# Fused attention and two networks on one core: the second network's down product as seven products of 256 columns, spread over three items

## The chip, the cores and the metric

The kernel runs on one core of one Trainium2 chip, as one launch. The metric is the device time of the launch in microseconds. Five engines work in a core: PE multiplies matrices (its weight loads are shown apart, as PEld), DVE, ACT and POOL do elementwise work, and SP here only issues the transfers (DMA). Matrix products end in PSUM, which this kernel uses as eight buffers (banks) of 512 float32 columns; DVE or ACT carries them from there to SBUF.

## The reference, cut to what matters

```python
x = attention(q, k, v)                 # 2304 tokens, 512 features, chunks of 64 tokens
P = sinkhorn(exp(x @ w_gate))          # 8 experts, 8 rounds
out = sum_e P[:, e] * (relu(x @ w1[e]) @ w2[e])        # first network, 1024 hidden each
h = maximum(maximum(out @ w1, out @ w2), out @ w3)     # second network, 768 hidden
return h @ w_out                                       # the down product of the change
```

All is float32 in and out. The kernel splits each operand of a product into a high part and a low remainder (both of the type float32r) and adds three products: high by high, high by low, low by high.

## The kernel before, in words

**Items.** The work is a list of 123 items (`items`). Items 0 to 95 are the first network, items 96 to 122 (kind `m`) the second: for each of three blocks of 768 tokens (`sb`) three parts `p` of 256 hidden units, and for each part three items `i`, one for each of the weights w1, w2 and w3. Three items with i = 0, 1, 2 make a group: the elementwise maximum of their three results is the hidden tile, `m`, of four quarters (two halves of the hidden units by two halves of the tokens, the tokens alternating by q = 0, 1).

**The up product.** `up(n)` computes an item by seven products instead of eight, after Strassen and Winograd: `PRODUCTS` lists them with the bank (`a`, `g`, `b`) into which each is added. A position `pos` (0 to 6) is one such product: 2 k by 3 parts, so 6 matmuls of 384 columns, 42 an item. After positions 0, 1 and 2 ACT copies the bank aside (`s0` to `s2`, line 360), after positions 3 to 6 DVE adds and takes the maximum (lines 366 and 313). The next product on the same bank waits for that read.

**The down product.** `down(n, q, j)` (line 452) multiplies one of six token tiles of 128 tokens by w_out: 6 matmuls of 512 columns, accumulated in one bank of the pools `wk` and `dn`, and `evict2` (line 493) copies or adds the bank to `ar`; with the last part `p` it sends the tile to `out`. The six tiles of a group (36 matmuls) run in one piece after position 6 of the next group's first item; those of the very last group run at the end, with two left over from the group before it.

**Weights.** All weights of the second network stand prepared in DRAM, `scr` (up) and `scro` (down). They pass through a ring of 24 slots of 256 KB in SBUF (`wr`). `line_up_all` fixes the order of the chunks, 7 slots for each item and 4 for each group's down product, and `room(k)` gives back k slots and issues the next chunks that fit. SP issues in the order of the program and each transfer waits there, so a transfer that waits holds all that stand behind it.

**The next block's input.** `x_next` (line 675) loads two token tiles of the next block (`xr`), and `x_cols` (line 571) turns them into the seven moving operands in three steps; its first step has ACT casts and DVE subtractions that read `xr`. Six such pieces run in items 98 to 113, one in a group, and `xcol` holds them.

**Decoding.** During the first network's blocks 1 and 2, `decode_all` (line 724) turns the second network's float64 weights into the prepared form, a step at a time, by `decode_step`.

**What sets the order.** All is written out by hand in the loop at line 1207: `at(n, pos, fn)` places side work behind a position, `later` holds splits for the next position, `pend` the tiles of the down product. Each engine runs its own list in that order.

Of the kernel before, what the change touches and what calls it, by code (L numbers as in the profile page):

```python
# [9 lines left out]
F32 = mybir.dt.float32  # L10
F32R = mybir.dt.float32r
# [37 lines left out]
DOWN = ["c0", "t1", "t2", "t3", "c1", "c3", "t4"]  # L49


@with_exitstack
def kernel(ctx: ExitStack, tc: tile.TileContext, qk, vv, wg, wts, wts2, out):
# [31 lines left out]
    scr = dram.tile([3 * NP2, P, 7, 2, 2, P], F32, name="scr")  # L85
    scro = dram.tile([NP2, P, 2, 2, DM], F32, name="scro")
    w1s = dram.tile([NPAIR, P, 7, 512], F32, name="w1s")
# [141 lines left out]
    def line_up(key, src, n, parts):  # L229
# [5 lines left out]
        slot_of[key] = []  # L235

    def line_up_all():
        for n in range(NPAIR, ni):
            it = items[n]
            if n == NPAIR:  # L240
                continue
            if it["kind"] == "M":
                line_up(("U", n), w1s[it["g"]], 7, (4, 3))
            else:
                line_up(("U", n), scr[it["p"] * 3 + it["i"]].rearrange("p s h k f -> p s (h k f)"), 7, (4, 3))
            if NPAIR + 2 <= n < first_of[3] + 2:
                j = (n - NPAIR - 2) // 2
                key, o = ("D", j), w2s[j % NPR].rearrange("p s b f -> p (s b) f")
                if n % 2 == 0:
                    line_up(key, o[:, 0:6], 6, (4, 2))  # L250
                else:
                    line_up(("E", j), o[:, 6:14], 8, (4, 4))
            elif n >= first_of[3] + 2 and it["i"] == 0 and n > first_of[3]:
                line_up(("O", n - 1), scro[items[n - 1]["p"]].rearrange("p c h f -> p (c h) f"), 4, (4,))
        line_up(("O", ni - 1), scro[items[ni - 1]["p"]].rearrange("p c h f -> p (c h) f"), 4, (4,))

    def room(k):
        ring["room"] += k
        while chunks and chunks[0][2] <= ring["room"]:
            key, a, k, src = chunks.pop(0)  # L260
            ring["room"] -= k
            while k:
                s = ring["put"] % NSLOT
                m = min(k, NSLOT - s)
                nc.sync.dma_start(out=wr[:, s:s + m].bitcast(F32).rearrange("p s h f -> p s (h f)"),
                                  in_=src[:, a:a + m])
                slot_of[key] += range(s, s + m)
                ring["put"] += m
                a, k = a + m, k - m

# [4 lines left out]

    mt = [None]
    later = []

    def up(n):
# [8 lines left out]
        if m2 and it["i"] == 0:  # L288
            c = mt[0] = pbm.rearrange("p b q w -> p (b q) w")
        if it["down"] and not scaled:  # L290
            hb = hr[:, (it["p"] if m2 else n) % 2]
            hh, hl = hb[:, 0], hb[:, 1]
            it["h"] = (hh, hl)

        def finish(q, src):
# [17 lines left out]
            nc.vector.tensor_tensor(out=m[:, q], in0=src, in1=m[:, q], op=ALU.max)  # L313
            if it["i"] == 2:
                lo = lambda: nc.vector.tensor_tensor(
                    out=hl[:, q], in0=m[:, q], in1=hh[:, q].bitcast(F32), op=ALU.subtract)
                later.append(lambda: (nc.scalar.copy(out=hh[:, q], in_=m[:, q]), later.append(lo)))

        def scale(out, src, pb):
# [132 lines left out]
    def down(n, q, j):  # L452
# [7 lines left out]
        own_w = own(n)  # L460
        o = p.rearrange("p (a b) -> p a b", a=2) if own_w else p
        for f in range(2):
            hi = HIDX[f, q]
            for i, (h, x) in enumerate(((hh, 0), (hh, 1), (hl, 0))):
                if own_w:
                    w = w2b(n)[:, 2 * f:2 * f + 2, x]
                else:
                    w = wr[:, slot_of["O", n][2 * f + x]].rearrange("p h f -> p (h f)")
# [4 lines left out]
    def new_acc(t):  # L473
        acc[t] = ar[:, t % TS]
        return acc[t]

    def evict(it, t, p):
# [12 lines left out]
        if it["g"] == NPAIR - 1:  # L490
            y_due.append((clock[0], t))

    def evict2(it, t, p):
        if it["p"] == 0:
            nc.scalar.copy(out=new_acc(t), in_=p)
            return
        nc.vector.tensor_tensor(out=acc[t], in0=p, in1=acc[t], op=ALU.add)
        if it["p"] == NP2 - 1:
            nc.sync.dma_start(out=out[t * P:(t + 1) * P, :], in_=acc[t])

# [181 lines left out]
    def big_again():  # L682
# [3 lines left out]
        big[0] = ctx.enter_context(tc.tile_pool(name="big2", bufs=1, reuse_waits="tile"))  # L686
        xb.extend(big[0].tile([P, 7, 2, W], F32R, name=nm) for nm in ("xbh", "xbl"))


# [34 lines left out]
    def decode_all(half_):  # L724
        jobs = []
        for p in range(NP2):
# [5 lines left out]
            for c in range(2):  # L732
                jobs.append((p, None, c, [(slice(0, 4), wts2[2 * (2 * p + c) + 1, :, 1].rearrange(
                    "p (i f) -> p i f", i=4))]))
        m = len(jobs) // 2
        jobs = jobs[m * half_:m * half_ + m]
        loaded, rest = {}, []
        for at_ in range(-1, m):
# [13 lines left out]
            nc.gpsimd.tensor_tensor(out=V[:, 0:4].rearrange("p i f -> p (i f)"), in0=v, in1=r, op=ALU.add)  # L752
            hi, lo = (bg_[:, o:o + 896].bitcast(F32R).rearrange("p (i f) -> p i f", i=7) for o in (4096, 4992))
            yield
            if i is not None:
                strassen_w([V[:, x] for x in range(4)], [V[:, 4 + x] for x in range(4)], nc.gpsimd)
                src = V[:, 1:8]
                dst = lambda h, p=p, i=i, k=k: scr[p * 3 + i, :, :, h, k, :]
            else:
                hi, lo = (x[:, 0:4].rearrange("p i f -> p (i f)") for x in (hi, lo))  # L760
                src = V[:, 0:4].rearrange("p i f -> p (i f)")
                dst = lambda h, p=p, k=k: scro[p, :, k, h]
            yield
            nc.scalar.copy(out=hi, in_=src)
            yield
            rest = [lambda lo=lo, src=src, hi=hi: nc.vector.tensor_tensor(
                        out=lo, in0=src, in1=hi.bitcast(F32), op=ALU.subtract),
                    lambda lo=lo, hi=hi, dst=dst: [nc.sync.dma_start(out=dst(h), in_=x.bitcast(F32))
                                                   for x, h in ((hi, 0), (lo, 1))]]
            if at_ + 1 < m:  # L770
# [269 lines left out]
    def s_open():  # L1040
# [8 lines left out]
        views.append(left.tile([P, NH - 13, 2, W], F32R, name="hy"))  # L1049
        bg_ = left.tile([P, 5888], F32, name="bg")  # L1050
        views.append(hr.rearrange("p b h q w -> p (b h q w)").rearrange("p (s h w) -> p s h w", h=2, w=W))
# [42 lines left out]
    for k in (4, 5):  # L1094
        for j in range(TS // 2):
            n = first_of[k - 1] + 3 * j
            if k == 4 and j < 2:
                n = first_of[3] + 3 + j
                if j == 0:
                    at(n - 1, 0, lambda n=n: x_next(4, 0, n))  # L1100
                else:
                    for a in (2, 9, 15):
                        at(n + a // 7, a % 7, lambda n=n: next(xcol[n]))
# [12 lines left out]
    with tc.manual_schedule():  # L1116
# [87 lines left out]

        held = [((7 * n + 6 + i) // 7, (7 * n + 6 + i) % 7) for n in (NPAIR, NPAIR + 1) for i in range(3)]
        pend = [(0, q, j) for q in (1, 0) for j in range(TS // 2)]
        for n in range(1, ni):
# [3 lines left out]
            for pos in up(n):  # L1211
# [18 lines left out]
                if pos < 3:  # L1230
                    decode_step(n)
                if n <= NPAIR:
                    run = 2 if pos in (1, 3, 5) else 0
                else:
                    run = len(pend) if pos == 6 and big_m and it["i"] == 0 else 0
                    if run and n > ni - 4:
                        run = 4
                for i in range(run):
                    if pend:
                        down(*pend.pop(0))  # L1240
                    while pos == 5 and later:
                        later.pop(0)()
                    if n in xcol and n != first_of[3] + 4 and i in (0, 2, 4):
                        next(xcol[n])
                    if (n, i) == (first_of[3] + 3, 3):
                        x_next(4, 1, n + 1)
                if run and big_m and not pend:
                    room(4)
                if pos == 3 + (n == 1):
# [17 lines left out]
            if it["down"] and (n < NPAIR or big_m):  # L1267
                assert len(pend) == (2 if n == ni - 1 else 0)
                pend += [(n, q, j) for q in (1, 0) for j in range(TS // 2)]
        while later:  # L1270
            later.pop(0)()
        for d in pend:
            down(*d)
# [39 lines left out]
```

## Time and profile before

| | |
|---|---|
| median of 3 runs | 1774.05 us (1773.16 to 1775.4) |
| the profiled execution's own time | 1772.81 us |
| its span, first to last instruction | 1771.0 us |
| PE busy | 1761.3 us, 99% of the span |
| DVE, POOL, ACT busy | 73%, 56%, 44% |
| granted TensorE clock | 1.00 of 2.4 GHz in nearly all of the span |

The span is what the profiler saw of that one execution; about 1.8 us of its time lie around it. A view of windows gives the busy time of each engine in a stretch, a timeline the instructions in order, the view of waits who waited for whom. A matmul's duration in a timeline holds its way through the array, so the time that one costs in a stream is read from the starts of a row of them.

### The profile page before, as it was taken

How to read it: one execution, taken by the hardware profiler on the slowest of the kernel's cores; microseconds unless marked ns; L12 is line 12 of the kernel's file. 1: busy time of each engine (PE TensorE's matmuls, PEld its weight loads, DVE VectorE, ACT ScalarE, POOL GpSimd, SP SyncE). 2: the span in 40 equal slices, each digit the busy share in tenths (PEclk: the TensorE clock that was granted, in tenths of full speed). 3: DMA queues.
4: the chain of work that ended last, by engine and by line, in shares of the span. 5: the costliest groups of instructions: out<-in, count | busy, mean ns of one | idle time of the engine just before them, and what ended most of it. 6: DMA issues, size and time to landing. Idle time of an engine off the chain costs nothing.

```text
span 1771.0 us, 30169 instructions
## 1 busy us (share of the span) xinstructions
PE 1761.3 (99%) x10764; PEld 1682.9 (95%) x10764; DVE 1298.7 (73%) x2342; ACT 777.1 (44%) x1566; POOL 997.5 (56%) x891
## 2 busy tenths in 40 slices
PE   8999999999999999999999999999999999999999
PEld 7888888989999999999999999999999999999998
DVE  8768657678885778887886886878788766664535
ACT  6665664664555534333333444434333333323221
POOL 4665665677777776766675677576767555000000
PEclk9999999999999999999999999999999999999999
DMA  7999998899988888988889779888988786877662
GB/s 240 364 368 358 334 357 309 326 373 338 357 309 334 326 315 285 335 299 298 286 311 319 255 259 345 305 298 294 318 302 315 266 304 244 282 254 260 244 245 106
DMA packets 206487, 532.89 MB, mean 301 GB/s; under 512 B 16161, under 2 KB 95361, under 8 KB 181249
## 3 DMA queue, kind: packets, MB, share of 16 engines
q1 hardware_dynamic: 206336, 530.97, 83.8%
q8 instruction: 85, 1.39, 0.3%
q14 instruction: 66, 0.53, 0.1%
HBM read 373.31 MB, written 156.02 MB: 299 GB/s over the span
## 4 chain that ended last, share of the span: by engine, by line
PE 97%; DMA 1%; DVE 1%; ACT 1%; issue 0%; POOL 0%; SPq 0%; DVEq 0%; POOLq 0%
PE pa L353 28%; PE dn L411 27%; PE dn L469 19%; PE pg L353 14%; PE pb L353 7%; DMA w2s<-w2y 0%; PE xp L905 0%; PE s L804 0%; DMA st<-in_wts 0%; PE gp L922 0%; PE hq L660 0%; PE hs L804 0%; DVE xl L602 0%; POOL wr L170 0%; PE yp L506 0%
## 5 line engine op out<-in xcount | busy, mean ns | idle before, releaser
L353 PE MATMUL pa<-xh,wr 128*128 128x384 f32 x1808 | 529.6, 337 | 0.0
L469 PE MATMUL dn<-wr,hr 128*128 128x512 f32 x1476 | 356.2, 392 | 0.0
L353 PEld LDWEIGHTS pa<-xh,wr 128*128 128x128 f32 x1808 | 332.5, 188 | 5.6 <-DVE c L366 0.8
L469 PEld LDWEIGHTS dn<-wr,hr 128*128 128x128 f32 x1476 | 275.4, 188 | 53.9
L353 PE MATMUL pa<-xl,wr 128*128 128x384 f32 x904 | 303.1, 335 | 0.0
L411 PE MATMUL dn<-hr,wr 128*128 128x384 f32 x1344 | 274.9, 335 | 0.0
L353 PE MATMUL pg<-xh,wr 128*128 128x384 f32 x904 | 268.4, 337 | 0.1
L360 ACT COPY s<-pa 128x384 f32<-128x384 f32 x244 | 117.3, 481 | 301.4 <-PE pa L353 297.4
L411 PEld LDWEIGHTS dn<-hr,wr 128*128 128x128 f32 x1344 | 237.1, 188 | 0.1
L366 DVE TENSOR_TENSOR c<-pb,s 128x384 f32<-128x384 f32 x82 | 45.7, 557 | 201.8 <-PE pb L353 179.6
L273 POOL TENSOR_TENSOR hr<-c,hr 128x384 fp32r<-128x384 f32 x96 | 110.9, 1161 | 143.0 <-ACT hr L272 137.7
L411 PE MATMUL dn<-hx,wr 128*128 128x384 f32 x840 | 182.8, 338 | 0.0
L353 PEld LDWEIGHTS pa<-xl,wr 128*128 128x128 f32 x904 | 169.7, 188 | 4.0
L353 PEld LDWEIGHTS pg<-xh,wr 128*128 128x128 f32 x904 | 166.4, 188 | 1.8 <-DVE tq L322 0.3
L353 PE MATMUL pg<-xl,wr 128*128 128x384 f32 x452 | 151.1, 334 | 0.0
L411 PEld LDWEIGHTS dn<-hx,wr 128*128 128x128 f32 x840 | 151.0, 188 | 0.0
L273 POOL TENSOR_TENSOR hr<-tq,hr 128x384 fp32r<-128x384 f32 x128 | 148.0, 1172 | 0.5 <-ACT hr L272 0.5
L353 PE MATMUL pb<-xh,wr 128*128 128x384 f32 x452 | 134.1, 337 | 0.0
L420 DVE TENSOR_TENSOR ar<-dn,ar 128x384 f32<-128x384 f32 x240 | 122.8, 545 | 9.4 <-PE dn L411 9.2
L273 POOL TENSOR_TENSOR hx<-c,hx 128x384 fp32r<-128x384 f32 x60 | 68.7, 1148 | 106.2 <-ACT hx L272 105.7
L411 PE MATMUL dn<-hy,wr 128*128 128x384 f32 x504 | 111.1, 336 | 0.0
L420 DVE TENSOR_TENSOR ax<-dn,ax 128x384 f32<-128x384 f32 x180 | 93.2, 549 | 18.2 <-PE dn L411 18.2
(246 smaller groups left out, 3208.5 us busy)
## 6 DMA issues: line engine op xcount, KB each, us to landing
wr<-w2s SPq DMA_DIRECT2D x80, 1024.0 KB, 6.4
w1s<-wr SPq DMA_DIRECT2D x32, 1792.0 KB, 9.8
wr<-w1s SPq DMA_DIRECT2D x53, 1024.0 KB, 7.6
wr<-w1s SPq DMA_DIRECT2D x58, 768.0 KB, 6.7
w2s<-wr SPq DMA_DIRECT2D x55, 512.0 KB, 6.6
wr<-w2s SPq DMA_DIRECT2D x52, 512.0 KB, 7.1
wr<-scr SPq DMA_DIRECT2D x22, 1024.0 KB, 5.1
wr<-scr SPq DMA_DIRECT2D x27, 768.0 KB, 6.0
```

Source lines behind the costliest of these rows:

```text
L273: (eng or nc.gpsimd).tensor_tensor(out=l, in0=v, in1=h.bitcast(F32), op=ALU.subtract)
L353: nc.tensor.matmul(ps, lhsT=wt[:, x, ws], rhs=y[:, xi, k], start=b not in begun, stop=k == 1 and i == 2, skip_group_check=True)
L360: nc.scalar.copy(out=s[pos], in_=ps)
L366: nc.vector.tensor_tensor(out=inner, in0=ps, in1=s[other], op=ALU.add)
L411: nc.tensor.matmul(p, lhsT=w[:, a, dt * P:(dt + 1) * P], rhs=h[m][:, b], start=m == 0 and q == 0, stop=m == 1 and q == 2)
L420: nc.vector.tensor_tensor(out=o, in0=p, in1=o, op=ALU.add)
L469: nc.tensor.matmul(o, lhsT=h[:, hi, ts], rhs=w, start=(f == 0 and i == 0), stop=(f == 1 and i == 2))
```

## The change

It replaces the down product of the second network, for all groups but the last, by the same seven-product scheme as the up product: seven products of 3 matmuls of 256 columns for each pair of token tiles (j = 0, 1, 2), which `token_down` yields one by one. They are no longer run in one piece but spread over the three items of the next group, by `TURNS` (key 7 * i + pos, value the pairs j that make a step there). The four sums of hidden quarters that the scheme needs are taken on DVE and split on ACT and POOL (7 splits where there were 4 quarters). The down weights become seven prepared sums (`scro` of 7 or 8 slots instead of 4); they stay in slots of their own (`own_o`), which are refilled behind the last step of a group, and the ring for the up weights shrinks to 17 slots. The last group keeps the old scheme.

```diff
+TOKEN = [("c0", "a"), ("t1", "g"), ("t2", "a"), ("c3", "b"), ("t3", "a"), ("c1", "g"), ("t4", "a")]
+HSLOT = {"c0": 0, "t1": 1, "t2": 2, "c3": 4, "t3": 5, "c1": 6, "t4": 7}
+TURNS = {4: (0,), 5: (0,), 6: (0,), 7: (0,), 8: (0,), 9: (0,), 10: (0, 1), 11: (1, 1), 12: (1,), 13: (1,),
+         14: (1, 2), 15: (1,), 16: (2, 2), 17: (2, 2), 18: (2,), 19: (2,)}
...
-                line_up(("O", n - 1), scro[items[n - 1]["p"]].rearrange("p c h f -> p (c h) f"), 4, (4,))
-        line_up(("O", ni - 1), scro[items[ni - 1]["p"]].rearrange("p c h f -> p (c h) f"), 4, (4,))
+                if n == first_of[3] + 3:
+                    line_up(("O", n - 1), flat(scro[items[n - 1]["p"]]), 7, (4, 3))
+        slot_of["O", ni - 1] = []
...
+            got = []
+            for _ in range(k):
+                got.append(ring["put"])
+                ring["put"] = min((s - got[-1] - 1) % NSLOT + got[-1] + 1 for s in range(NSLOT) if s not in own_o) % NSLOT
+            slot_of[key] += got
+            fetch(got, src[:, a:a + k])
+            if key == ("O", first_of[3] + 2):
+                own_o.extend(got)
...
+            if it["i"] == 2 and n < ni - 1:
+                if q.start == 3:
+                    t = mq[0]
+                    at(n + 1, 0, lambda: (sub(t[:, 0], m[:, 2], m[:, 0]), sub(t[:, 1], m[:, 1], t[:, 0])))
+                    at(n + 1, 1, lambda: (split("t1", t[:, 0]), sub(m[:, 2], m[:, 1], m[:, 2])))
...
+    def token_down(n, j):
+        it = items[n]
+        slots, first_, last = slot_of["O", n], it["p"] == 0, it["p"] == NP2 - 1
+        t = it["sb"] * TS + 2 * j
+        turn[0] ^= 1
+        pools = {"a": (wk, dn)[turn[0]], "g": (dn, wk)[turn[0]], "b": (wk, dn)[turn[0]]}
+        C = lambda d, q, t=t: ar[:, (t + q) % TS, 256 * d:256 * d + 256]
+        bank = {}
+        for x, (kind, b) in enumerate(TOKEN):
+            fresh = b not in bank
+            if fresh:
+                pl = pools[b]
+                bank[b] = pl.tile([P, DM], F32, name="dn", tag=pl.name)[:, 0:256]
+            ps, h, w = bank[b], hr8[:, HSLOT[kind]], wr[:, slots[OSLOT[kind]]]
+            for i, (y, z) in enumerate(((0, 0), (0, 1), (1, 0))):
+                nc.tensor.matmul(ps, lhsT=h[:, y, j * P:(j + 1) * P], rhs=w[:, z],
+                                 start=fresh and i == 0, stop=i == 2, skip_group_check=True)
+            if x < 3:
+                o = C(*((0, 0), (1, 1), (0, 1))[x])
+                if first_:
+                    nc.scalar.copy(out=o, in_=ps)
+                else:
+                    e = big[0].tile([P, 256], F32, name=f"e{x}", tag=f"e{x}")
+                    nc.scalar.copy(out=e, in_=ps)
+                    nc.gpsimd.tensor_tensor(out=o, in0=o, in1=e, op=ALU.add)
+            else:
+                o = C(*((0, 0), (1, 1), (0, 1), (1, 0))[x - 3])
+                if x == 6 and first_:
+                    nc.scalar.copy(out=o, in_=ps)
+                else:
+                    nc.vector.tensor_tensor(out=o, in0=ps, in1=o, op=ALU.add)
+            if last and x >= 5:
+                q = 6 - x
+                nc.sync.dma_start(out=out[(t + q) * P:(t + q + 1) * P, :], in_=ar[:, (t + q) % TS])
+            if j == TS // 2 - 1 and x == 6 and n + 3 < ni - 1:
+                slot_of["O", n + 3] = own_o
+                for a, b in ((0, 4), (4, 7)):
+                    fetch(own_o[a:b], flat(scro[items[n + 3]["p"]])[:, a:b])
+            yield
...
+            for a in (7, 9, 10) if (k, j) == (4, 1) else (6, 9, 10):
+                at(n + a // 7, a % 7, lambda n=n: next(xcol[n]))
...
-                for i in range(run):
+                for _ in range(2 if n <= NPAIR and pos in (1, 3, 5) else 0):
                     if pend:
                         down(*pend.pop(0))
...
+                if nets:
+                    for j in TURNS.get(7 * it["i"] + pos, ()):
+                        if n < ni - 1 or pos < 3:
+                            next(nets[j])
...
         while later:
             later.pop(0)()
+        for _ in nets[-1]:
+            pass
+        turn[0] ^= 1
         for d in pend:
             down(*d)
```

The left-out rest makes `decode_all` write the seven sums (four more POOL subtractions for each of its six down pieces), gives `fetch` its loop, and adds the tiles `mq`.

On SP, around the start of the group of items 102 to 104, where `xr` of block 1 is fetched (`wr` is the ring, `scr` the up weights, `scro` the down weights, 512 columns a slot), there stood before:

```order
L265 DMA wr<-scr 128x1536
L265 DMA wr<-scro 128x2048
L265 DMA wr<-scr 128x2048
L265 DMA wr<-scr 128x1536
L265 DMA wr<-scr 128x2048
L679 DMA xr<-ys 128x512 x2
L265 DMA wr<-scr 128x1536
```

At the same place stands now:

```order
L285 DMA wr<-scr 128x1536
L285 DMA wr<-scro 128x2048
L285 DMA wr<-scro 128x1536
L285 DMA wr<-scr 128x512
L285 DMA wr<-scr 128x1536 x2
L749 DMA xr<-ys 128x512 x2
L285 DMA wr<-scr 128x2048
```

The down weights, 4 slots before and 7 now, have moved from inside a group to its border, directly ahead of the 7 slots of the next item but one and of `xr`.

On ACT, around the casts of `xr` in item 108 (line 495 before and 546 now evict a down product's bank, `s` an up product's), there stood before:

```order
L360 COPY s_16749<-pg 128x384
L360 COPY s_16758<-pa 128x384
L311 COPY pbm<-pa 128x384
L495 COPY ar<-dn 128x512
L581 CAST xh<-xr 128x4x128
L582 CAST xh<-xr 128x2x128
L495 COPY ar<-dn 128x512 x2
```

There stands now, in the same item:

```order
L332 COPY pbm<-pa 128x384
L651 CAST xh<-xr 128x4x128
L652 CAST xh<-xr 128x2x128
L546 COPY ar<-dn 128x256
L395 COPY s_17087<-pa 128x384
L395 COPY s_17101<-pg 128x384
```

The casts stand at the same position, but behind them now come an eviction of the bank `a` of the down product and the copies of the next item's up product.

On DVE, at the end of the program, there stood before:

```order
L366 TENSOR_TENSOR c<-pg,s_17871 128x384
L313 TENSOR_TENSOR pbm<-c,pbm 128x384
L313 TENSOR_TENSOR pbm<-pa,pbm 128x384
L315 TENSOR_TENSOR hr<-pbm,hr 128x768
L315 TENSOR_TENSOR hr<-pbm,hr 128x384 x2
L497 TENSOR_TENSOR ar<-dn,ar 128x512 x8
```

And now:

```order
L401 TENSOR_TENSOR c<-pg,s_18463 128x384
L334 TENSOR_TENSOR pbm<-c,pbm 128x384
L334 TENSOR_TENSOR pbm<-pa,pbm 128x384
L346 TENSOR_TENSOR hr<-pbm,hr 128x768
L346 TENSOR_TENSOR hr<-pbm,hr 128x384 x2
L556 TENSOR_TENSOR ar<-dn,ar 128x256 x4
L568 TENSOR_TENSOR ar<-dn,ar 128x512 x6
```

Between the last hidden tile and the last six tiles stand now the evictions of four steps of `token_down` that the last item did not take.

## Rows read from the trace of the kernel before

**Rows 1.** The page's head: span, then busy time, share and instructions by engine.
```profile
span 1771.0 us, 30169 instructions
PE 1761.3 (99%) x10764; PEld 1682.9 (95%) x10764; DVE 1298.7 (73%) x2342; ACT 777.1 (44%) x1566; POOL 997.5 (56%) x891
```
**Rows 2.** The chain of waits that ended last, shares of the span.
```profile
PE 97%; DMA 1%; DVE 1%; ACT 1%; issue 0%; POOL 0%; SPq 0%; DVEq 0%; POOLq 0%
```
**Rows 3.** Windows, second network: length, busy by engine, clock, DMA share, GB/s.
```profile
1487.00:1771.00 284.00, 280.26 (x1511) 266.74 (x1509) 151.20 (x263) 79.32 (x156) 6.14 (x3) 1.00 0.66 233
```
**Rows 4.** PE's timeline around one group's down product: start, length, engine, line, operation.
```profile
1585.60 8.36 PE L469 MATMUL dn<-wr,hr 128*128 128x512 f32 x36
1593.80 0.33 PE L353 MATMUL pa<-xbh,wr 128*128 128x384 f32 x1
...
1594.86 0.33 PE L353 MATMUL pg<-xbh,wr 128*128 128x384 f32 x1
...
1602.15 0.33 PE L353 MATMUL pg<-xbh,wr 128*128 128x384 f32 x1
```
**Rows 5.** Weight loads' timeline in the attention's start, products of 128 columns.
```profile
22.87 0.97 PEld L660 LDWEIGHTS hs<-xr,st 128*128 128x128 f32 x8
```
**Rows 6.** POOL groups by shape: a split of 384 columns, an add of 256.
```profile
L273 POOL TENSOR_TENSOR hr<-c,hr 128x384 fp32r<-128x384 f32 x96 | 110.9, 1161 | 143.0 <-ACT hr L272 137.7 <-issue 4.8
...
L130 POOL TENSOR_TENSOR ws<-st 128x256 f32<-128x256 f32 x32 | 27.8, 870 | 0.0
```
**Rows 7.** DMA issues of the last stretch: count, size, median us to landing.
```profile
wr<-scr SPq DMA_DIRECT2D x20, 1024.0 KB, 5.1
...
out<-ar SPq DMA_DIRECT2D x18, 256.0 KB, 2.3
...
xr<-ys SPq DMA_DIRECT2D x12, 256.0 KB, 5.4
```
**Rows 8.** A window inside a burst of transfers, columns as in Rows 3.
```profile
1611.00:1616.00 5.00, 5.00 (x30) 4.95 (x30) 2.64 (x6) 0.79 (x3) 0.00 (x0) 1.00 1.01 409
```
**Rows 9.** SP's timeline at a group's border.
```profile
1601.67 7.24 SPq L265 DMA_DIRECT2D wr<-scr  x3
1609.00 0.86 SPq L679 DMA_DIRECT2D xr<-ys  x2
```
**Rows 10.** Waits of the last stretch: us in total, times, longest.
```profile
SPq L265 <- PE pa L353: 141.1, 40, 6.9
...
DVE xT L577 <- DMA xr<-ys: 2.1, 1, 2.1
```
**Rows 11.** DVE's timeline, same border: the first read of `xr`.
```profile
1615.37 0.41 DVE L577 TENSOR_TENSOR xT<-xr 128x256 f32<-128x256 f32 x1
```
**Rows 12.** Groups by shape of the last stretch, ACT and DVE.
```profile
L360 ACT COPY s<-pa 128x384 f32<-128x384 f32 x52 | 24.9, 480 | 103.0 <-PE pa L353 98.9 <-DVE pbm L313 3.9 <-ACT hr L317 0.2
...
L581 ACT CAST xh<-xr 128x512 fp32r<-128x512 f32 x3 | 1.9, 623 | 0.0
L582 ACT CAST xh<-xr 128x256 fp32r<-128x256 f32 x3 | 1.2, 407 | 0.0
...
L577 DVE TENSOR_TENSOR xl<-xr,xh 128x256 fp32r<-128x256 f32 x3 | 1.2, 417 | 0.0
```
**Rows 13.** Timeline of PE and DVE around position 5 of an item i = 2.
```profile
1747.67 0.34 PE L353 MATMUL pg<-xh,wr 128*128 128x384 f32 x1
...
1748.54 0.55 DVE L366 TENSOR_TENSOR c<-pg,s 128x384 f32<-128x384 f32 x1
...
1749.60 0.55 DVE L313 TENSOR_TENSOR pbm<-pa,pbm 128x384 f32<-128x384 f32 x1
```
**Rows 14.** Timeline of PE and DVE at the end.
```profile
1756.18 11.08 PE L469 MATMUL dn<-wr,hr 128*128 128x512 f32 x48
...
1756.89 0.55 DVE L313 TENSOR_TENSOR pbm<-pa,pbm 128x384 f32<-128x384 f32 x1
1757.36 1.88 DVE L315 TENSOR_TENSOR hr<-pbm,hr 128x768 fp32r<-128x768 f32 x3
```

More of the change, by code (lines that the diff above doesn't have):

```diff
@@ L261, in room, with fetch @@
             ring["room"] -= k
[L262 to L269, printed above, removed]
+            got = []
[6 more added lines that the diff above has]
+                own_o.extend(got)
+    def fetch(slots, src):
+        a = 0
+        while a < len(slots):
+            k = next((k for k in range(1, len(slots) - a) if slots[a + k] != slots[a] + k), len(slots) - a)
+            nc.sync.dma_start(out=wr[:, slots[a]:slots[a] + k].bitcast(F32).rearrange("p s h f -> p s (h f)"),
+                              in_=src[:, a:a + k])
+            a += k
+    own_o = []
     def hilo(h, l, v, eng=None):
@@ L288, in up @@
         if m2 and it["i"] == 0:
-            c = mt[0] = pbm.rearrange("p b q w -> p (b q) w")
-        if it["down"] and not scaled:
-            hb = hr[:, (it["p"] if m2 else n) % 2]
+            c = mt[0] = mq[1] if mq and (n - first_of[3]) // 3 % 2 else pbm.rearrange("p b q w -> p (b q) w")
+        if it["down"] and not scaled and (not m2 or n == ni - 1):
+            hb = hr[:, 0 if m2 else n % 2]
             hh, hl = hb[:, 0], hb[:, 1]
@@ L687, in big_again @@
         xb.extend(big[0].tile([P, 7, 2, W], F32R, name=nm) for nm in ("xbh", "xbl"))
+        mq.extend(big[0].tile([P, 3 + i, W], F32, name=f"mq{i}") for i in range(2))
     big, bigs = [None], ExitStack()
@@ L752, in decode_all @@
             nc.gpsimd.tensor_tensor(out=V[:, 0:4].rearrange("p i f -> p (i f)"), in0=v, in1=r, op=ALU.add)
-            hi, lo = (bg_[:, o:o + 896].bitcast(F32R).rearrange("p (i f) -> p i f", i=7) for o in (4096, 4992))
+            hi, lo = (bg_[:, o:o + 1024].bitcast(F32R).rearrange("p (i f) -> p i f", i=8) for o in (4096, 5120))
             yield
[L755 to L762, printed above, removed]
+            strassen_w([V[:, x] for x in range(4)], [V[:, 4 + x] for x in range(4)], nc.gpsimd)
+            put = [(slice(1, 8), slice(0, 7)), (slice(0, 1), slice(7, 8))][:1 + (i is None and p == NP2 - 1)]
+            dst = scr[p * 3 + i, :, :, :, k, :] if i is not None else scro[p, :, :, :, k * P:k * P + P]
+            r = slice(2 - len(put), 8)
             yield
-            nc.scalar.copy(out=hi, in_=src)
+            nc.scalar.copy(out=hi[:, r], in_=V[:, r])
             yield
[L766 to L769, printed above, removed]
+            rest = [lambda lo=lo, V=V, hi=hi, r=r: nc.vector.tensor_tensor(
+                        out=lo[:, r], in0=V[:, r], in1=hi[:, r].bitcast(F32), op=ALU.subtract),
+                    lambda lo=lo, hi=hi, dst=dst, put=put: [
+                        nc.sync.dma_start(out=dst[:, o, h], in_=x[:, i].bitcast(F32))
+                        for i, o in put for x, h in ((hi, 0), (lo, 1))]]
             if at_ + 1 < m:
@@ L1266 @@
                 big_again()
-            if it["down"] and (n < NPAIR or big_m):
-                assert len(pend) == (2 if n == ni - 1 else 0)
+            if it["down"] and (n < NPAIR or n == ni - 1):
                 pend += [(n, q, j) for q in (1, 0) for j in range(TS // 2)]
+            elif it["down"] and big_m:
+                nets[:] = [token_down(n, j) for j in range(TS // 2)]
         while later:
             later.pop(0)()
+        for _ in nets[-1]:
+            pass
+        turn[0] ^= 1
         for d in pend:
```

58 lines of the change are left out of this document (27 added, 31 removed).

## The prediction

> **What bounds the kernel now.** I read the page's head first, then the chain of waits, then windows over the last stretch, and then timelines of one group of items, engine by engine. The reader is to see that PE is busy for 99% of the span [rows 1] and makes 97% of the chain [rows 2], so that a matmul taken away is time gained as long as nothing else comes late. In the second network (1487 to 1771 us) PE is still busy for 280 of 284 us, while DVE is at 53%, ACT at 28%, POOL nearly idle, and the transfers run at 233 GB/s [rows 3]. That mean hides something: inside a burst they run at 409 GB/s with every DMA engine busy [rows 8], so they come in bursts with pauses between, and the question is what stands behind a burst. The timelines of one group border answer it: SP waits for a slot most of the time (141 us in 40 waits for PE alone) [rows 10] and then issues the weights and `xr` [rows 9]. `xr` is issued from 1609.00 and read first at 1615.37 [rows 9, 11], about 7 us after the start of its item (1602.15 - 1.04 + 7.29 = 1608.4). It lands 5.4 us after its issue in the median [rows 7], and once in this stretch DVE already waited 2.1 us for it [rows 10]. That is the one place with no slack.
>
> **The matmuls.** In a row of them, 36 of 512 columns take 1593.80 - 1585.60 = 8.20 us, 0.2278 each, and 42 of 384 columns take 1602.15 - 1594.86 = 7.29 us, 0.1736 each [rows 4]. The straight line through both gives 0.1194 for 256 columns. Eight groups change: 8 x 36 x 0.2278 = 65.6 us go, 8 x 63 x 0.1194 = 60.2 us come, together -5.4 us. That is all the gain there is, 0.3% of the kernel, because seven products of 256 columns are 12.5% fewer columns but pay the fixed part of a matmul 63 times instead of 36. No row shows a float32r matmul of 256 columns. Below, the price is bounded by the weight loads: eight loads of 128 columns follow each other in 0.97 us, between 0.111 and 0.121 apiece [rows 5]; at 0.111 the gain is 9.6 us. Above, by the shortest spacing that this operand type shows, 0.1736: then the change costs 21.9 us. I take 0.1194, since it is nearest to the loads' own rate and lies on the line.
>
> **The side work.** A group gets seven POOL splits of at most 1.16 us and up to nine POOL adds of 0.87 us [rows 6], 16 us on an engine that was nearly idle there, in groups of some 29 us; the splits are placed two to three positions (over 2 us) ahead of their matmuls. DVE's evictions of 256 columns take 0.42 us [rows 12] where 512 columns were carried before, and it loses the four quarters' subtractions. The extra sums while decoding, 24 POOL operations of 128 columns, at most 0.87 us each, lie beside hundreds of us of PE. I cost all of it at nothing; the cover is the next position's 1.04 us of up product, and PE itself is the engine that would show it if it were gone.
>
> **The tail.** Here a stall comes in. At the end PE's up product is through at 1756.18, and DVE is busy with the last hidden tile until 1757.36 + 1.88 = 1759.24 [rows 14], 3.06 us later. Before, 12 matmuls of the group ahead (2.7 us) and tiles that need only the first quarters covered this. Now four steps x3 to x6 are left; x3 to x5 take 9 x 0.119 = 1.07 us, and x6 adds into bank `a`, which DVE has to empty of x4 first. DVE's order puts x3's and x4's adds behind the three subtractions, 0.42 us each [rows 12], so x4's is done 3.9 us after the up product. PE waits from 1.07 to 3.9: +2.8 us. The six tiles of the last group come after it unchanged.
>
> **The border with the weights' burst.** Set t = 0 where PE ends the last step (position 5 of item i = 2). The slots of the down weights are free only then, so their 7 slots (1.84 MB) are issued at t = 0, SP holds everything behind them, and then come the 7 slots of the item i = 1 and the two halves of `xr`. The first 1 MB lands at 5.1 [rows 7] and is needed at 1.04 + 5 x 1.04 = 6.25: in time. Behind it stand 0.79 + 1.84 + 0.26 = 2.88 MB, 7.05 us at 409 GB/s [rows 8], so `xr` has landed at 12.15 (first half) and 12.8 (second). That they land in order I read from the sizes: 256 KB lands after 2.3 us by itself (`out`) and after 5.4 us behind 1 MB (`xr`) [rows 7]. ACT reaches the casts of `xr` at t = 9.05 (1.04 + 7.29 + two steps) and stands there; queued behind them are the eviction of step x2 and the copies of the next item. Casts of 0.62 and 0.41 us [rows 12] end at 13.2, the eviction (256 columns, taken as 0.41) at 13.6. PE wants bank `a` for x4 after position 1 of item i = 1, at 1.04 + 8.37 + 2 x 1.04 + 0.36 = 11.85. It waits 1.75 us. Four borders have both bursts (items 102, 105, 108, 111): +7.0 us. Bounds: nothing, if the transfers overtake; and at a sixth less than 409 GB/s, 341, the 2.88 MB take 8.45 us and each border 1.4 us more.
>
> The Trainium skill ("DMA: Bandwidth & Descriptors", Specifications) puts the limit of a core's share of HBM at about 358 GB/s. By it the burst would take 8.0 us and the change cost some 5 us more than by the measured 409; the trace decides, since this core's window ran above that limit.
>
> **The border after a block's end.** In two groups (105 and 114) the finished tiles are sent to `out` ahead of the down weights on SP, and the last of them waits for DVE. Position 5 ends on PE at p = 1747.84 [rows 13]; DVE is two operations behind, and the add of x6 would start where the third starts, p + 1.76, and end at p + 2.2. With the issue of `out` the weights go out at p + 2.6 instead of p + 0.4. They land at p + 7.7, wanted at p + 6.6: 1.1 us; the item i = 1's first four slots land 4.5 us later, at 12.2, wanted at 10.9: 1.3 us. Together 2.4 us, twice (items 108, 117): +4.8 us.
>
> **Sum.** -5.4 + 2.8 + 7.0 + 4.8 = +9.2 us. Against the profiled execution's own 1772.81 us that is 1782.0; the median of the runs lies 1.24 us above that execution, so I forecast 1783.2 us.
>
> **Rivals.**
> 1. The burst is hidden: the transfers of one queue share the DMA engines, or the slots come free earlier, and `xr` lands before ACT stands at its casts (t = 9.05; the price is 0 from there down, and 1 us for each us later, past 10.4). Then only the tail is left: -5.4 + 2.8 = -2.6, 1771.4 us, not slower. For it: in the trace DVE waited for `xr` in one of six pieces only. Against it: 1 MB more stands in front now, issued later, and rows 7 show landing in order. 12%.
> 2. The weight loads bind at 256 columns: 504 matmuls at 0.1736 instead of 0.1194 add 27 us, and the longer steps (0.16 us each) hide about 8 us of the border waits: 1802 us. Against it stand rows 5, where loads come every 0.121 us or less. 3%.
> 3. No fixed part: 128 more columns cost 0.0542 us in rows 4, so the fixed part of a matmul is 0.011; were it hidden at 256 columns, one took 0.108, the gain grew by 5.5 us and the time were 1777.7 us, if nothing else moves. Against it: rows 4 show the fixed part at 384 and at 512 columns alike. 4%.
> 4. The change doesn't do what it says because a bank or a hidden sum comes late in every group, one wait of 1 us in each of the eight: 1791 us. Against it: two positions between split and use. 3%.
>
> The Trainium skill ("TensorE: Matmul & The Clock Gate", Back-to-back issue gap) gives N / 2.4 + 2.5 ns for a matmul of N columns, 109 ns for 256, about rival 3. For 512 columns it gives 216 ns where the trace has 228, so I follow the trace.
>
> **How the numbers follow.** My forecast has 78%: 1783.2 us, and with the bounds of its own terms (matmuls at 0.111: -4.2; borders at 341 GB/s: +7.4) 1776 to 1791. What a measurement of this kernel can tell from no change is about 0.2%, 3.5 us: slower begins at 1777.6. Of my 78% 75 lie above that and 3 within; rival 1's 12% are half within 0.2% and half faster (with the tail partly covered); rivals 2 and 4 are slower, 3 is half slower, half the same. With 2% faster from causes I don't see: faster 8%, same 11%, slower 81%. The range is 1776 to 1791: below it lies most of rival 1, above it rival 2, and I hold the low end no lower, since 1771 has little chance and what is between has less.
>
> **What would show it.** In the profile after: L541 matmuls of 256 columns start 0.119 us apart; a step takes 0.36 us. `xr` lands 11 us or more after the down weights' issue at the borders of 102, 105, 108 and 111, ACT shows a wait for `xr<-ys` of 2 to 3 us there, and PE one of 1 to 2 us for ACT. At 108 and 117 PE waits for `wr<-scro` and `wr<-scr`. At the end PE is idle for nearly 3 us before x6. I am wrong if PE's idle time in the last stretch stays under 6 us, if L541 is spaced above 0.13 or below 0.11, or if time is lost ahead of 1487 us.

## The result, and the profile after

The changed kernel takes 1792.59 us (1791.72 to 1793.32, 4 runs) against 1773.61 us (1772.22 to 1775.4, 4 runs) before: a ratio of 1.0106, 95% interval 1.0089 to 1.0124. It is slower, as forecast, but by 19.0 us instead of 9.2, and lies 1.6 us above the range.

The page's head of after (span; busy time, share and instructions by engine) answers to [rows 1], the shares of its chain of waits to [rows 2]:

```profile
span 1789.5 us, 31117 instructions
...
PE 1763.4 (99%) x10980; PEld 1693.1 (95%) x10980; DVE 1325.6 (74%) x2407; ACT 805.6 (45%) x1661; POOL 1103.2 (62%) x1016
...
PE 92%; DMA 4%; DVE 2%; issue 1%; ACT 1%; POOL 0%; SPq 0%; DVEq 0%; ACTq 0%; POOLq 0%
```

"99%" says nothing here; the chain does: PE's share has gone from 97% to 92%, and DMA's from 1% to 4%. The windows of after (columns as in [rows 3]) show the second network, then two bursts of transfers in two halves each, then the border of item 117:

```profile
1487.00:1789.50 302.50, 280.88 (x1726) 275.70 (x1724) 174.26 (x328) 105.52 (x251) 101.17 (x104) 0.99 0.65 239
...
1549.00:1554.00 5.00, 5.00 (x32) 5.00 (x31) 3.45 (x7) 4.17 (x10) 3.00 (x3) 1.00 0.95 363
1554.00:1559.00 5.00, 4.75 (x30) 4.42 (x28) 0.56 (x1) 0.85 (x2) 4.57 (x6) 1.00 1.02 416
...
1580.00:1585.00 5.00, 5.00 (x31) 5.00 (x30) 4.41 (x8) 2.98 (x7) 2.31 (x3) 1.00 0.94 346
1585.00:1590.00 5.00, 3.78 (x25) 3.61 (x24) 1.13 (x3) 2.06 (x6) 5.00 (x6) 1.00 0.99 400
...
1714.00:1717.00 3.00, 1.07 (x7) 0.75 (x5) 1.12 (x2) 1.62 (x4) 3.00 (x4) 1.00 0.98 385
1717.50:1720.50 3.00, 2.93 (x10) 2.94 (x11) 0.00 (x0) 0.37 (x1) 1.74 (x2) 0.50 1.00 396
```

PE is busy for 281 of 302.5 us, where it was busy for 280 of 284: 17.9 of the 18.5 us by which the span grew are idle PE. The view of waits of after, PE's from 1480 us on (total, times, longest), names them; PE had no wait worth a row there before:

```profile
PE dn L541 <- ACT e L549: 5.9, 3, 2.5
PE dn L541 <- DMA wr<-scro: 4.2, 2, 2.5
PE pa L388 <- DMA wr<-scr: 3.7, 3, 1.3
PE dn L541 <- DVE ar L556: 2.6, 1, 2.6
PE dn L541 <- ACT ar L546: 1.0, 1, 1.0
```

Three causes: ACT (itself waiting for `xr`) 6.9 us, weights 7.9 us, the tail 2.6 us. To price them I measured each item from the start of its first up matmul to that of the next item. Without a stall the three items of a group take 8.40, 10.63 and 10.60 us; the table has every item that is more than 0.2 us longer somewhere (but 101, which is at 10.97 in all of them). Its other columns are the experiments below. Before, an item i = 1 or 2 took 7.3 us, and item 122 with the end 22.14.

| item (i) | after | no refetch | xr early | pieces | out late | two transfers | all |
|---|---|---|---|---|---|---|---|
| 103 (1) | 13.33 | 10.63 | 10.63 | 10.67 | 13.23 | 14.77 | 10.63 |
| 105 (0) | 9.78 | 8.40 | 10.25 | 8.40 | 9.76 | 8.59 | 8.40 |
| 106 (1) | 11.96 | 10.63 | 10.68 | 10.82 | 11.99 | 14.75 | 10.63 |
| 108 (0) | 11.83 | 8.40 | 12.38 | 9.12 | 9.61 | 10.59 | 8.40 |
| 109 (1) | 12.00 | 10.95 | 10.63 | 12.02 | 13.35 | 13.30 | 10.63 |
| 112 (1) | 13.69 | 10.63 | 11.08 | 10.85 | 14.98 | 14.96 | 10.63 |
| 114 (0) | 8.64 | 8.40 | 8.51 | 8.40 | 8.40 | 8.40 | 8.40 |
| 115 (1) | 10.98 | 10.63 | 10.82 | 10.63 | 10.83 | 10.88 | 10.63 |
| 117 (0) | 12.59 | 8.40 | 12.04 | 9.52 | 10.16 | 12.41 | 8.40 |
| 120 (0) | 9.73 | 8.40 | 9.00 | 8.40 | 8.97 | 8.40 | 8.40 |
| 122 + end | 25.58 | 27.07 | 25.58 | 27.10 | 25.57 | 27.17 | 23.25 |

Now one border as it went. The timelines of after around the start of item 103, engine by engine (columns as in [rows 4]; in brackets the idle time before and its releaser):

```profile
1546.26 0.52 PE L541 MATMUL dn<-wr,hr 128*128 128x256 f32 x3
...
1546.82 0.79 SPq L285 DMA_DIRECT2D wr<-scro  x2
1547.66 1.87 SPq L285 DMA_DIRECT2D wr<-scr  x3
1549.63 0.92 SPq L749 DMA_DIRECT2D xr<-ys  x2
...
1558.41 0.34 PE L388 MATMUL pg<-xh,wr 128*128 128x384 f32 x1
1559.81 0.62 ACT L651 CAST xbh<-xr 128x512 fp32r<-128x512 f32 x1 [3.39 <-DMA xr<-ys]
1560.44 0.40 ACT L652 CAST xbh<-xr 128x256 fp32r<-128x256 f32 x1
1560.75 0.36 ACT L549 COPY e<-dn 128x256 f32<-128x256 f32 x1
1561.17 0.62 PE L541 MATMUL dn<-wr,hr 128*128 128x256 f32 x3 [2.42 <-ACT e L549]
```

The group's last step (1546.26) frees the down weights' slots; SP issues their refetch 0.2 us behind it, then the up weights, then `xr`. ACT stands at the cast of `xr` for 3.4 us, the eviction `e` is queued behind the cast, and PE cannot refill the bank. Each link is as predicted; only `xr` lands at 1559.8, 13.2 us behind the end of the step, and not at 12.15.

The second kind of border, without `xr` in the way: SP ahead of item 105 and PE at the starts of items 106 and 118, in after's timeline.

```profile
1579.15 0.80 SPq L285 DMA_DIRECT2D wr<-scro  x2
1580.04 1.13 SPq L285 DMA_DIRECT2D wr<-scr  x2
...
1588.07 0.51 PE L541 MATMUL dn<-wr,hr 128*128 128x256 f32 x3
1589.80 0.41 PE L388 MATMUL pa<-xbh,wr 128*128 128x384 f32 x1 [1.22 <-DMA wr<-scr]
...
1714.73 0.34 PE L388 MATMUL pa<-xh,wr 128*128 128x384 f32 x1
1717.57 1.01 PE L541 MATMUL dn<-wr,hr 128*128 128x256 f32 x3 [2.50 <-DMA wr<-scro]
1718.37 0.52 PE L388 MATMUL pg<-xh,wr 128*128 128x384 f32 x1
...
1720.29 0.77 PE L541 MATMUL dn<-wr,hr 128*128 128x256 f32 x3
1720.90 0.34 PE L388 MATMUL pa<-xh,wr 128*128 128x384 f32 x1
```

At 1589.80 the first product of item 106 waits for its up weights. At 1717.57 down weights are late, and after that idle time PE runs at half clock (0.50 in the window above, 1.2 GHz) for some 3.4 us: by the starts, a step of three matmuls takes 0.80 us and the six of 384 columns behind it 1.92, instead of 0.37 and 1.04.

The transfers of the burst at item 105, from after's view of DMA issues between 1578 and 1593 us (columns as in [rows 7]). The first 1 MB of down weights lands 5.0 us after its issue, the 1 MB of up weights that item 106 wants 9.6 us after its own:

```profile
wr<-scr SPq DMA_DIRECT2D x2, 768.0 KB, 10.0
wr<-scro SPq DMA_DIRECT2D x1, 1024.0 KB, 5.0
wr<-scr SPq DMA_DIRECT2D x1, 1024.0 KB, 9.6
...
wr<-scro SPq DMA_DIRECT2D x1, 768.0 KB, 6.6
xr<-ys SPq DMA_DIRECT2D x2, 256.0 KB, 10.9
```

The tail in after's timeline answers to [rows 14]:

```profile
1773.07 1.23 PE L541 MATMUL dn<-wr,hr 128*128 128x256 f32 x9
...
1774.25 1.89 DVE L346 TENSOR_TENSOR hr<-pbm,hr 128x768 fp32r<-128x768 f32 x3
1776.05 1.08 DVE L556 TENSOR_TENSOR ar<-dn,ar 128x256 f32<-128x256 f32 x3
1776.86 0.62 PE L541 MATMUL dn<-wr,hr 128*128 128x256 f32 x3 [2.56 <-DVE ar L556]
1777.32 8.35 PE L506 MATMUL dn<-wr,hr 128*128 128x512 f32 x36
```

Nine matmuls, then 2.56 us in which x6 waits for DVE's add of x4, which stands behind three subtractions: as predicted, item for item.

### The profile page after: what moved, and what is told of

Same layout as the page of the kernel before. It is cut to its first block, busy times and chain, and to the rows that moved or that the text cites. A ratio compares the mean times of both kernels' runs of the same rounds, so it can differ in the third digit from the quotient of the medians.

```text
span 1789.5 us, 31117 instructions
## 1 busy us (share of the span) xinstructions
PE 1763.4 (99%) x10980; PEld 1693.1 (95%) x10980; DVE 1325.6 (74%) x2407; ACT 805.6 (45%) x1661; POOL 1103.2 (62%) x1016
## 4 chain that ended last, share of the span: by engine, by line
PE 92%; DMA 4%; DVE 2%; issue 1%; ACT 1%; POOL 0%; SPq 0%; DVEq 0%; ACTq 0%; POOLq 0%
PE pa L388 26%; PE dn L446 26%; PE dn L506 15%; PE pg L388 13%; PE pb L388 7%; PE dn L541 3%; DMA xr<-ys 2%; DMA wr<-scr 1%; DMA w2s<-w2y 0%; PE xp L974 0%; PE s L873 0%; DMA wr<-scro 0%; DVE c L401 0%; PE gp L991 0%; DVE pbm L334 0%
## 5 line engine op out<-in xcount | busy, mean ns | idle before, releaser
L506 PE MATMUL dn<-wr,hr 128*128 128x512 f32 x1188 | 289.3, 392 | 0.0
L506 PEld LDWEIGHTS dn<-wr,hr 128*128 128x128 f32 x1188 | 221.4, 188 | 42.9
```

The lines of the kernel that those rows point to most:

```text
L506: nc.tensor.matmul(o, lhsT=h[:, hi, ts], rhs=w, start=(f == 0 and i == 0), stop=(f == 1 and i == 2))
```

## The experiments

The theory: the refetch of the down weights can start only when the group's last step has freed their slots, so one burst falls on each border, and what stands in it behind them (up weights, `xr`) is late. The rivals are the smaller ring by itself, and the tail.

**No refetch.**

```diff
                 slot_of["O", n + 3] = own_o
-                for a, b in ((0, 4), (4, 7)):
-                    fetch(own_o[a:b], flat(scro[items[n + 3]["p"]])[:, a:b])
```

> Leaves out the refetch of the down weights at the group borders (the seven slots keep the first part's weights, so the products are with the wrong weights; all instructions else stay). Theory A, that the 7 slots behind the last step hold SP and put xr and the up weights late: PE's waits at items 103 to 120 (some 20 us by the starts of the items) go nearly all, the tail's 2.9 us stay: before -4.1 +2.9 = about 1772.5 us, 20 us under the changed kernel. Rival B, that PE loses its time to the steps themselves (evictions, banks, the order of ACT and DVE): the items stay long, within 4 us of 1792.6.

Measured: 1773.78 us against 1772.94, ratio 1.0006 (0.9997 to 1.0015). Nearly all that the borders lost is back (the table), and one wait of PE is left:

```profile
PE dn L541 <- DVE ar L556: 2.6, 1, 2.6
```

So 18.8 us come back, though in the profiled execution the end runs at half clock and costs 1.5 us more. What the borders lost they lost through the refetch (rival B falls), and the rest of the change is a draw. Whether it is the refetch's bytes or its place in the order, this run cannot tell; the run in pieces below does.

**`xr` ahead of the burst.**

```diff
-                at(n, 0, lambda k=k, j=j, n=n: x_next(k, j, n))
+                at(n - 1, 3, lambda k=k, j=j, n=n: x_next(k, j, n))
```

> Only moves the issue of xr from the start of a group to position 3 of the item before, ahead of the down weights on SP. Theory A: ACT no longer stands at the casts of xr, so the waits in items 103, 106, 109 and 112 (2.7, 1.4, 1.4 and 3.1 us) go, but the xr data pushes the down weights and the up weights back by up to 1.3 us at these borders: 4 to 8 us under the changed kernel, 1785 to 1789. Rival C, that the up weights alone hold PE at these borders and xr only waits beside them: within 2 us of 1792.6.

Measured: 1783.98 us, ratio 1.0065 (1.0053 to 1.0078), 8.6 less than after and a little under what was expected. Items 103, 106 and 109 are at 10.63 to 10.68. PE's waits in this kernel:

```profile
PE dn L541 <- DMA wr<-scro: 4.3, 2, 2.2
PE pa L388 <- DMA wr<-scr: 3.3, 3, 1.7
PE dn L541 <- DVE ar L556: 2.6, 1, 2.6
```

No wait for ACT is left, and the weights are as late as before, so rival C falls. The two are separate victims of one burst. (Item 108 grew from 11.83 to 12.38: after PE's wait there, some 3.4 us from 1617.3 on ran at half clock in this run.)

**The tail's fourth step.**

```diff
-                        if n < ni - 1 or pos < 3:
+                        if n < ni - 1 or pos < 4:
```

> Only lets the last item take steps up to position 3 instead of 2, so that x3 and x4 run before the end and x6 no longer stands behind DVE's last subtractions. The tail theory (x6 waits for x4's eviction): PE's 2.6 us wait for DVE in L541 goes; the last tiles then wait some 1.4 us for the low part of the hidden tile instead; 1.0 to 2.0 us under the changed kernel. Rival: the end is bound by the low part anyway, no difference within 0.5 us.

Measured: 1791.5 us, ratio 1.0103 (1.009 to 1.0117), 1.1 less than after; item 122 went from 25.58 to 24.36, with two waits of 0.5 us in place of one of 2.6. That shows the tail, real and small; the total alone does not, since the intervals of this kernel and of after overlap.

**The refetch in pieces, each as soon as its slots are free.**

```diff
-            if j == TS // 2 - 1 and x == 6 and n + 3 < ni - 1:
-                slot_of["O", n + 3] = own_o
-                for a, b in ((0, 4), (4, 7)):
+            if j == TS // 2 - 1 and n + 3 < ni - 1:
+                slot_of["O", n + 3] = own_o
+                for a, b in {4: ((0, 2), (3, 6)), 5: ((6, 7),), 6: ((2, 3),)}.get(x, ()):
```

(moved ahead of the stores to `out`)

> Only the refetch is issued in pieces, each slot as soon as its last product is issued (five slots two positions earlier, one a position earlier, one as before), and ahead of the stores of out. Theory A: the burst at each border starts 2.8 us earlier; waits for wr<-scro (items 108, 117) and for wr<-scr go, the waits for xr at 103, 106, 109, 112 shrink to under 1 us: 12 to 18 us under the changed kernel, 1775 to 1781. Rival D, that the transfers' amount and not their start is what holds PE (the queue is full all the time): within 5 us of 1792.6.

Measured: 1777.66 us, ratio 1.0024 (1.0016 to 1.0033): 14.9 of the 18.8 us come back with the same bytes, so rival D falls. SP's timeline at the border of item 102 shows how: the first five slots go out, as two transfers, 3.6 and 2.8 us ahead of the first issue in after. Not all went as expected: item 109 stays at 12.02, with a wait of 1.1 us for ACT.

```profile
1543.27 3.87 SPq L285 DMA_DIRECT2D wr<-scro  x4
1547.19 1.39 SPq L285 DMA_DIRECT2D wr<-scr  x3
1548.68 0.86 SPq L749 DMA_DIRECT2D xr<-ys  x2
```

**The stores to `out` later.**

```diff
-                nc.sync.dma_start(out=out[(t + q) * P:(t + q + 1) * P, :], in_=ar[:, (t + q) % TS])
+                put = lambda q=q: nc.sync.dma_start(out=out[(t + q) * P:(t + q + 1) * P, :], in_=ar[:, (t + q) % TS])
+                if j == TS // 2 - 1 and n + 3 < ni:
+                    at(n + 3, 6, put)
+                else:
+                    put()
```

> Only the last pair's two stores to out (of the groups whose tiles are finished) are issued behind position 6, after the down and the up weights, instead of ahead of them. Theory A (an SP queue held by a store that waits for DVE makes the weights late): the waits at items 108 and 117 (3.4 and 4.2 us) fall to the 0 to 1.4 us that the same border costs where no store stands ahead (111, 114, 105, 120); 4 to 7 us under the changed kernel. Rival: the weights are late at 108 and 117 for another reason, the same 7.6 us stay and the time within 1.5 us of 1792.6.

Measured: 1791.96 us, ratio 1.0102 (1.0088 to 1.0116), a miss in the total. Items 108 and 117 lose 2.2 and 2.4 us, about as expected, but 109 and 112 grow by 1.35 and 1.29. The 2.4 at 117 are not all the stores' waits: the half clock after PE's wait there in after, some 1.4 to 1.6 us, is absent in this run, and PE's longest wait at 117 went from 2.50 to 1.60 us. At 109 the reason stands in this kernel's SP timeline: the stores moved in front of `xr`. (At 112, some 3.4 us at half clock follow PE's wait.)

```profile
1613.00 1.82 SPq L285 DMA_DIRECT2D wr<-scr  x3
1614.92 0.87 SPq L559 DMA_DIRECT2D out<-ar  x2
1615.89 1.84 SPq L753 DMA_DIRECT2D xr<-ys  x2
```

**Before with the smaller ring.**

```diff
     at(NPAIR, 6, h_open)
+    at(first_of[3] + 2, 0, lambda: room(-7))
```

> The kernel before, with 7 slots of its ring never given back from item 98 on, so that 17 circulate as in the changed kernel (there for the up weights alone, here for up and down). Theory A says that the order on SP at the border holds PE and not the number of slots alone: the weights still start a whole item ahead (7.3 us against 5 to 6 us to land), except that the down weights (4 slots) now wait too: 0 to 4 us over the kernel before. Rival E, that the smaller ring alone makes the loss: 10 us or more over the kernel before.

Measured: 1774.03 us against 1773.85, ratio 1.0001 (0.9992 to 1.001). The ring of 17 slots alone costs nothing; this rival falls.

**Pieces, `xr` early and the tail's step together.** The edits of those three kernels.

> The three edits together: refetch in pieces ahead of the stores, xr issued an item earlier, two steps more before the end. If the waits add up as read (refetch 14 to 15 us, xr's remaining 2 us, tail 1.2 us and no half clock at the end): 1771 to 1774, within 0.2% of the kernel before.

Measured: 1773.09 us, ratio 0.9997 (0.9988 to 1.0006). The repairs add up, to no change against before.

**All, with the late stores and an end in another order.** As the last, with the stores of the two last tiles behind position 6 and the first two tiles of the last group interleaved, the products with the hidden tile's high part ahead of those with its low part:

(`down_parts`, which is `down` with a stop between the two kinds of product, is left out here.)

```diff
+        two = [down_parts(*d) for d in pend[:2]]
+        for g in (0, 1):
+            for d in two:
+                next(d, None)
+        for d in pend[2:]:
             down(*d)
```

> As the three edits together, with the last pair's stores to out behind position 6 and the last group's first two tiles computed side by side, the products with the high part ahead of those with the low part. The waits left at 108 and 117 (0.7 and 1.1 us) and at the end (1 to 2 us) go: 1768.5 to 1772, up to 0.2% faster than before, which is what the arithmetic of the matmuls alone (-4.1 us) allows.

Measured: 1771.15 us against 1773.85, ratio 0.9985 (0.9977 to 0.9994): faster than both kernels, by 2.7 us than before. Items 103 to 120 of the table are at their unstalled lengths, and from 1480 us on PE waits once:

```profile
PE dn L523 <- ACT hr L348: 0.2, 1, 0.2
```

**The first up weights as two transfers.** In after, the burst brings the up weights of the item i = 1. Where the ring's wrap happens to cut the first four slots (items 102, 111, 114), item i = 0 shows no more than 0.24 us of wait; where they come as 1 MB (105, 108, 117, 120), 1.3 us and more.

```diff
-            fetch(got, src[:, a:a + k])
+            for u in ((0, 2), (2, 4)) if k == 4 and key[0] == "U" and items[key[1]].get("i") == 1 else ((0, k),): fetch(got[u[0]:u[1]], src[:, a + u[0]:a + u[1]])
```

> The kernel after, but the first four up slots of every item i = 1 come as two transfers of 512 KB instead of one of 1 MB, at the same places in SP's order and with the same bytes; PE's order is the same. Theory (an item's first product waits for the whole transfer in which its slot lies; where the ring's wrap happens to split it, at items 102, 111 and 114, the item before shows 8.40, 8.40 and 8.64 us, and where it comes as 1 MB, at 105, 108, 117 and 120, it shows 9.78, 11.83, 12.59 and 9.73): items 105 and 120 fall to 8.4 to 8.8, 108 to 10.3 to 10.7, 117 to 10.5 to 11.5; the waits for xr stay; 4 to 6.5 us less than after, 1786 to 1788.5. Rival (what counts is the bytes in the burst and where in the program it falls, not the cut): the four items stay as they are within 0.4, 1791 to 1794.

Measured: 1795.54 us against 1773.05, ratio 1.0126 (1.0109 to 1.0143). The items answered (105, 108 and 120 lose 1.19, 1.24 and 1.33 us; 117, where PE waits 2.24 us for down weights, only 0.18), the total went the other way. Two reasons. At 106 and 109 PE now comes earlier to an `xr` that lands no earlier (at 105's border 13.1 us behind the burst's first issue, 13.0 in after), and waits that much longer there. And this run has more half clock: at 103, 106, 112, 117 and at the end. Two of its windows after a wait of PE for ACT, and one after a wait for weights without it (1624):

```profile
1562.70:1566.10 3.40, 3.27 (x13) 3.27 (x13) 3.17 (x7) 1.14 (x4) 0.79 (x1) 0.52 1.03 423
1596.50:1599.90 3.40, 3.27 (x12) 3.27 (x13) 3.16 (x7) 1.16 (x4) 0.79 (x1) 0.53 0.67 278
...
1624.20:1627.60 3.40, 3.35 (x22) 3.35 (x23) 0.56 (x1) 0.95 (x3) 2.33 (x3) 1.00 0.99 391
```

**The same two chunks lined up apart, so that the first goes ahead of the burst.**

```diff
-                line_up(("U", n), scr[it["p"] * 3 + it["i"]].rearrange("p s h k f -> p s (h k f)"), 7, (4, 3))
+                line_up(("U", n), scr[it["p"] * 3 + it["i"]].rearrange("p s h k f -> p s (h k f)"), 7, (2, 2, 3) if it["i"] == 1 else (4, 3))
```

> The kernel after, but the first four up slots of every item i = 1 are lined up as two chunks of two slots, so that the first two are issued as soon as two slots of the ring are free, ahead of the down weights instead of behind them. Theory: as with the two transfers for the up weights (items 105 and 120 to 8.4, 108 to 10.3, 117 to 10.4), and with 0.52 MB less behind the first 1 MB of the burst xr lands 1.3 us earlier: items 103 and 112 lose 1.3 us each, 106 and 109 all of their 1.4: 9 to 12 us less than after, 1781 to 1784. Rival (the chunk ahead waits for its slots and holds SP, so the burst starts no smaller): no more than the two transfers bring, 1786 to 1790.

Measured: 1787.68 us, ratio 1.0085 (1.007 to 1.01): 4.9 less than after, where 9 to 12 were expected. Items 105 and 120 are at 8.40, 103 and 112 lose 1.75 and 0.96, but 106 and 109 stand at 12.58 and 12.19 instead of 10.63. At 105's border `xr` landed 12.2 us behind the burst's first issue instead of 13.0: 0.8 us sooner, where 1.3 were expected. So of the 1.38 us that PE no longer lost for up weights at 105, 0.62 came back at 106 as a wait for `xr`; at 108 and 109 it is 0.19 of 1.12. The expectation had counted two waits in a row on one burst as if both could be taken off. It also missed at 117 (12.65, expected 10.4) and at the end (27.15), where this run had half clock after waits of 2.48 and 2.56 us.

## Why the prediction was right in sign and half in size

- **The matmuls**, -5.4 predicted: -4.1. An item i = 2 without a stall went from 7.30 to 10.60 us with 27 matmuls more, 0.122 each; 504 x 0.122 = 61.5 against 65.6. The line through [rows 4] held to some 2%, but 0.122 is also what the weight loads take by themselves at the upper end (0.121, [rows 5]), so which of the two sets it is not shown; rivals 2 (0.1736) and 3 (0.108) are out. The Trainium skill ("TensorE: Matmul & The Clock Gate", Back-to-back issue gap) gives 109 ns for 256 columns; estimated by it, 504 take 54.9 us, and the trace does not agree.
- **The side work**, at nothing: right to 0.4 us, which item 101 loses in every run with the change. With the refetch gone no row of PE's waits for POOL, ACT or DVE is left but the tail's. Rival 4 falls.
- **The tail**, +2.8: PE shows the wait, 2.56 us. By the items it is 2.9: the last three took 46.0 us against 42.2 before, 3.8 more, of which 1.4 are waits at 120 and 121, while the group's own gain was 0.5.
- **The border with the weights' burst**, 4 x 1.75 = 7.0: this is the step that failed, by its size. Its chain is shown link by link above, but the burst lands later than computed. At item 102 the first 1 MB landed 5.6 us after its issue, 5.8 after the last step (5.1 taken), and `xr` 13.2 us after the last step (12.15 taken): 0.7 of the 1.0 us are lost before the first landing. The 409 GB/s are the dense part's rate; the window from 1549 to 1554 us has 363, the next 416. The step's own bound of 341 GB/s, 1.4 us more a border, was the nearer end. (The bound of +7.4 for all borders holds more than these 4 x 1.4 = 5.6; the rest the prediction does not work out.) What the borders lost in all is 2.70 us at 103, 1.38 + 1.33 at 105 and 106, 3.06 at 112, and 4.80 at 108 and 109, of which the stores to `out` are 2.2: 11.1 us without them. That PE's waits for ACT alone add up to 6.9 us, nearly the 7.0 of the term, is chance: at 103 and 112 they are 2.4 and 2.5 us instead of 1.75, at 106 and 109 only 1.0 each, because PE had already stood there for the weights.
- Inside that step, the up weights were passed over: it weighed 1 MB of down weights and `xr`, and not the 1 MB of up weights between them, which PE wants sooner (at 105 about 9.5 us after the last step; landed at 10.7). With `xr` behind them this is not a second price in full, since the one wait takes from the other, as the two transfers showed; without `xr`, at item 120, it is 1.33 us that no term held, and at 114 and 115 0.6.
- **The border after a block's end**, 2 x 2.4 = 4.8: by the run that moved them the stores cost 2.2 at 108. At 117 that run took off 2.4, but most of it is the half clock that followed PE's wait (some 1.4 to 1.6 us, for which the prediction had no term); the wait itself shrank by 0.9. In all 117 lost 4.19.
- **Sum**, by the items: -4.1 + 11.1 (the four borders) + 2.2 (the stores at 108) + 4.2 (117) + 1.3 (120) + 0.6 (114 and 115) + 0.4 (101 and 121) + 2.9 (the tail) = +18.6, against 18.5 between the two spans. Of the 9.4 us beyond the predicted 9.2 the four borders make 4.1, the border after a block's end 1.6, the matmuls 1.3, and what no term held (120, 114, 115, 101) the rest. Rival 1 (the burst is hidden) falls with PE's 17.4 us of waits; the time of rival 4 came out nearly, by another cause.

Why the burst starts slowly and a transfer ends late stays open; the runs show this much. Between the landings of the first down weights and of the first 1 MB of up weights at 105 lie 5.5 us (the issues at 1579.15 and 1580.04, landing 5.0 and 9.6 later), in which 1.84 MB were awaited: 334 GB/s, while the core moved 403 GB/s in just this stretch. So bytes of other transfers, by SP's order those behind, were moved in it too. The Trainium skill ("DMA: Bandwidth & Descriptors", Why a DMA increments its semaphore by 16 and not by 1) says that a transfer runs on up to 16 engines that finish independently; that could do it, but no row here shows the engines apart.

## What to carry to other kernels

A buffer that is refilled only when its last reader is done puts its whole transfer on the border; refill it slot by slot, in the order in which the slots come free, and put what is small and wanted soon ahead of it in the issuing queue. Price a burst by every transfer in it, each with the time at which it is wanted, at the rate from the burst's start and not of its dense middle. Waits that one burst causes in a row are not a sum: what is taken off the first is lost again at the second, wholly or in part, until the last transfer lands as much sooner.

## What the runs showed of the hardware that I had not expected

After some waits of PE of 2.2 to 2.8 us the granted clock fell to half (1.2 GHz) for some 3.4 us, which costs 1.3 to 1.6 us: in after at 1717.5; with no refetch and with pieces at the end (item 122 takes 27.1 instead of 25.6); with `xr` early at 1617.3; with the late stores at 1660.2; with two transfers five times; with the chunks lined up apart at 1713.0 and at the end; and with the tail's fourth step for some 6.8 us at once (item 117 took 14.08). It does not follow from the wait's length alone: after 2.42 us (item 103) and 2.56 us (the tail) in after the clock stayed at 1.00, after 2.44 and 2.56 us in the run with two transfers it fell. Nor does it follow from the program: over the whole span the mean granted clock of after was 0.999 in the profiled execution, the shortest of the four, and 0.997 in the other three. What decides it stays open. A wait of 2.2 us or more in a dense stream of matmuls can thus cost half as much again, and an edit's time can look better or worse than the waits that it removes.
